# First MLP's short token block: high and low inputs side by side in one product of 512 columns

## Chip, cores and metric

The kernel runs on one core of a Trainium2 chip. The metric is the device time of one execution in microseconds (us). The kernel before was timed three times: 840.6 us median, 839.95 lowest, 841.95 highest.

## What is computed

The inputs are q, k, v of 4 batches, 8 heads, 576 positions and 64 channels, and four weight matrices. Retention comes first; its output is 2304 tokens by 512 channels. Two MLPs follow, each with 2048 hidden units and no bias. Cut to what matters:

```
scores = (q @ k.T) / 8                      # per batch and head
ret    = scores * decay                     # gamma[h] ** (i - j) for i >= j, else 0
x      = (ret @ v), heads side by side      # [2304, 512]
h = x @ w_in;   g = softplus(h);               x = g @ w_out     # first MLP, 512 -> 2048 -> 512
h = x @ w_in2;  g = h * sigmoid(1.702 * h);  out = g @ w_out2    # second MLP
```

Everything is float32. TensorE gets each operand as a high part (the value rounded to float32r) and a low part (what the rounding left), and a product of two operands is the sum of three: high times high, low times high, high times low.

## The kernel before

**Blocks and slices.** The first MLP goes over five blocks of tokens: the first 512 tokens of batches 0, 1 and 2, then a short block `"t"` of 256 tokens (the last 64 of each of the four batches), then the first 512 of batch 3. A block goes over 16 slices of 128 hidden units. Below, "slice n" is slice n of the short block, 0 to 15, unless another block is named.

**One slice** (`run_first`, L213 to L292). `mm1` makes the slice's hidden values `ph` (128 hidden units by the block's tokens, one PSUM bank, two of them in turn): four steps `kd` over the 512 channels, and in each the three products high weight by high input, low weight by high input, high weight by low input. ScalarE takes softplus of `ph` into `g` (L260, a tile with one buffer), casts it to the high part `gh` (L265, helper at L94), and VectorE makes the low part `gl = g - gh` (L267, helper at L99). `mm2` multiplies the slice into the block's four output banks `y` (four steps `e`, three products each, in the order high-high, high-low, low-high). All these products are issued at L211.

**Order.** The order of the instructions of each engine is written out by hand (`tc.manual_schedule`), and each engine takes its instructions in that order. With LAG = 2 one pass of the loop at L269 is: `mm1` of slice n, `start` (softplus), then `mm2` of slice n - 2, within which the cast to `gh` of slice n stands after step e = 0 and `gl` of slice n after e = 2. Where a block begins (slice 0), the inputs are first split into `xh` and `xl` (`split_block`, four casts on ScalarE, then four subtractions on VectorE), and one more `mm2` of the block ahead runs in front of the first `mm1`. So in the order of TensorE, `mm1` of slices 14 and 15 of the short block is followed by `mm2` of 13 and 14, and then by the first `mm1` of batch 3's block.

**Side work.** Four times in a pass, `side()` (a small accumulator; `pre`, ending at L1267, sets its rates) lets other work issue one step: in `mm1` after kd = 1 and after kd = 3, in `mm2` after e = 1 and after e = 3. In the short block this is `sums_steps` (L744 on), which prepares the second MLP's weights: a unit reads 512 KB of weights, forms four sums and stores 1024 KB of high and low parts. It has four steps: **A**, two 256-column sums on VectorE (L728, L729 or L736, L737); **B**, two more (L730, L731 or L738, L739), the issue of the read two units ahead, and the cast of the first two sums on ScalarE; **C**, their low part on VectorE and the cast of the other two; **D**, the low part of those and the issue of the store by SyncE. The rate is 0.66 steps a call, so two units take three slices. Their order against the slices repeats every three slices. Each tile of these steps (`whole`, `sum`, `sum_halves`) has two buffers, so a cast in B waits for the store of two units ago to land. In slice 15 the rate is 0.

- Between the `gl` of slices 3, 6, 9, 12 and that of the slice behind them stand C and D ahead of `start`, and A behind it.
- Between the `gl` of slices 4, 7, 10, 13 and the next stand B and C ahead of `start`, and D behind it.
- Between the `gl` of slices 5, 8, 11 and the next stand A and B ahead of `start` (C follows the next `gl`).

**End of a block.** `done` (L1273 to L1279) copies each `y` bank out of PSUM, alternately on ScalarE and VectorE, and SyncE stores it. For the short block this happens in `mm2` of its slice 15, which runs right after `mm1` of slice 1 of batch 3's block.

```python
    for i, cur in enumerate(work):           # L269, shortened to the steady case
        g = start(cur, mm1(cur))
        for e in mm2(behind.pop(0)):
            if e == 0:
                rest = split(cur, g)
            if e == 2:
                rest()
            if e in (1, 3):
                side()
```

Of the kernel before, what the change touches and what calls it, by code (L numbers as in the profile page):

```python
# [7 lines left out]
F32 = mybir.dt.float32  # L8
F32R = mybir.dt.float32r
U32 = mybir.dt.uint32  # L10
AF = mybir.ActivationFunctionType
ALU = mybir.AluOpType
# [3 lines left out]
P = 128  # L16
T = 512
C0 = 256
ENDS = 320
LAG = 2  # L20
# [13 lines left out]
def kernel(  # L34
# [36 lines left out]
    nc = tc.nc  # L71
# [5 lines left out]
    KD = DM // P  # L77
# [8 lines left out]
    xp = ctx.enter_context(tc.tile_pool(name="xp", bufs=1))  # L86
    tp = ctx.enter_context(tc.tile_pool(name="tp", bufs=1))
# [4 lines left out]
    def hi(eng, dst, src):  # L92
        if eng == "a":
            nc.scalar.copy(dst, src)  # L94
        else:
            nc.vector.tensor_copy(dst, src)

    def lo(dst, src, h):
        nc.vector.tensor_tensor(out=dst, in0=src, in1=f32(h), op=ALU.subtract)  # L99
# [108 lines left out]
    def passes(out_ap, pairs, first, last):  # L208
        k = len(pairs)
        for i, (l, r) in enumerate(pairs):  # L210
            nc.tensor.matmul(out_ap, l, r, start=first and i == 0, stop=last and i == k - 1)  # L211

    def run_first(work, ws, get_x, side, done, pre, post):  # L213

        ts, ys = {}, {}
        behind, late = [], []

        def mm1(it):  # L220
            key, n, f = it
            xh, xl = get_x(key)
            w = ws(f, 0)
            ph = ps_h.tile([P, T], F32, tag="h", name="ph")
            for kd in range(KD):
                wh, wl = (w[:, j, kd * P:(kd + 1) * P] for j in range(2))
                passes(
                    ph[:, 0:n],
                    [(wh, xh[:, kd, 0:n]), (wl, xh[:, kd, 0:n]), (wh, xl[:, kd, 0:n])],
                    kd == 0, kd == KD - 1)  # L230
                if kd % 2:
                    while late:
                        late.pop()()
                    side()
            return ph[:, 0:n]

        def mm2(it):
            key, n, f = it
            w = ws(f, 1)
            gh, gl = ts.pop(it)  # L240
            first, last = f == 0, f == NF - 1
            if first:
                ys[key] = [ps_y.tile([P, T], F32, tag="y", name="y") for _ in range(KD)]
            for e in range(KD):
                c = slice(e * P, (e + 1) * P)
                wh, wl = w[:, 0, c], w[:, 1, c]
                for i, pair in enumerate([(wh, gh), (wh, gl), (wl, gh)]):
                    passes(ys[key][e][:, 0:n], [pair], first and i == 0, last and i == 2)
                    if i < 2:
                        yield None  # L250
                if last:
                    done(key, n, e, ys[key][e])
                yield e
            if last:
                ys.pop(key)
            post(key, f)

        def start(it, ph):
            g = tp.tile([P, T], F32, tag="g", name="g", bufs=1)[:, 0:it[1]]
            nc.scalar.activation(g, ph, AF.Softplus)  # L260
            return g

        def split(it, g):
            gh, gl = (tp.tile([P, T], F32R, tag="gg", name=nm, bufs=2 * LAG + 2)[:, 0:it[1]] for nm in ("gh", "gl"))
            hi("a", gh, g)  # L265
            ts[it] = gh, gl
            return lambda: lo(gl, g, gh)  # L267

        for i, cur in enumerate(work):  # L269
            pre(*cur)  # L270
            behind.append(cur)
            if cur[2] == 0 and i:
# [3 lines that stand above are left out]
                late.append(split(cur, start(cur, mm1(cur))))  # L276
                continue
            g = start(cur, mm1(cur))
            if i == len(work) - 1:
                split(cur, g)()  # L280
                continue
            if len(behind) <= LAG:
                late.append(split(cur, g))
                continue
# [7 lines that stand above are left out]
        return (step for it in behind for step in mm2(it))  # L292

    with tc.manual_schedule():
# [3 lines left out]
        tokens = {k: B * TAIL if k == "t" else T for k in order}  # L298
# [12 lines left out]
        xs = {}  # L311

        def x_tiles(key, layer):
            xs[layer, key] = [xp.tile([P, KD, T], F32R, tag="x8", name=g, bufs=2) for g in ("xh", "xl")]

        def split_x(key, layer, src, kd, cols=None):

# [6 lines left out]
        def split_block(key, layer, src):  # L324
            x_tiles(key, layer)
            for late in [split_x(key, layer, src, kd) for kd in range(KD)]:
                late()
# [4 lines left out]
        with ExitStack() as consts, ExitStack() as right, ExitStack() as second:  # L332
# [297 lines left out]
            for _ in range(WARM):  # L630
# [3 lines left out]
                out=mask[:, 0:2, :].rearrange("p u j -> p (u j)"), in_=mask[:, 0:2, :].rearrange("p u j -> p (u j)"),  # L634
# [33 lines left out]
            w1_gen = convert_first(units, slots, w1_raw, w1_tiles, w1_loaded, made)  # L668

            x_tiles(order[0], 1)  # L670
            for i, _ in enumerate(first_batch()):
                if i == 9:
# [10 lines left out]
            def side():  # L683
                for s in (side_gen, conv):
                    s["acc"] += counts.pop(0) if counts and s is conv else s["rate"]
                    while s["acc"] >= 1.0:
                        s["acc"] -= 1.0
                        next(s["g"], None)
# [580 lines left out]
            def post(key, f):  # L1269
                if key == order[-1] and 3 <= f < NF - 2:  # L1270
                    next(loads)

            def done(key, n, e, y):  # L1273
                c = e % 2 * n if 2 * n <= T else 0
                if not c:
                    y_out["t"] = tp.tile([P, T], F32, tag="yb", name="yb", bufs=3)
                yb = y_out["t"][:, c:c + n]
                hi("v" if e % 2 else "a", yb, y[:, 0:n])
                nc.sync.dma_start(out=y1[key][e], in_=yb)  # L1279

            work = [(k, tokens[k], f) for k in order for f in range(NF)]
            run_second(run_first(work, w1, lambda k: xs[1, k], side, done, pre, post))


# [74 lines left out]
```

## Time and profile before

| what | value |
|---|---|
| median of three runs (lowest, highest) | 840.6 us (839.95, 841.95) |
| the profiled execution's own time | 840.94 us |
| its span, first to last instruction | 839.2 us |
| TensorE busy | 826.9 us, 99% of the span |
| VectorE, ScalarE, GpSimd busy | 569.1, 401.2, 94.9 us (68%, 48%, 11%) |
| mean granted TensorE clock | 0.998 |
| DMA, mean over the span | 259 GB/s |

Busy times are of one profiled execution, whose own time is 0.34 us above the median of the runs; between its span and its time lie 1.7 us. The short block is worked on from about 327 to 381 us of the span. "Idle before" in a row is the time that the engine stood still just ahead of the instruction, with the instruction or transfer that ended it. Matmul rows overlap, since matmuls are pipelined: their pace is read from one start to the next.

### The profile page before, as it was taken

What the parts mean: (1) busy time and instruction counts of PE and PEld (TensorE: products, weight loads), DVE (VectorE), ACT (ScalarE), POOL (GpSimd) and SP (SyncE); (2) the same over time, 40 slices, a digit from 0 to 9 for tenths busy, and PEclk for the clock granted to TensorE, in tenths of its full rate; (3) what the DMA queues carried; (4) which work ended last, traced back from release to release, by engine and by line L of the source; (5) the groups of instructions that cost most, each with busy time, mean ns of one, the idle gap of its engine ahead of it and who ended that gap; (6) DMA issues with size and microseconds to landing.
All of it is one profiled execution on the core that took longest, in us unless ns stands there. A gap on an engine that the chain in (4) does not pass through costs nothing.

```text
span 839.2 us, 17129 instructions
## 1 busy us (share of the span) xinstructions
PE 826.9 (99%) x6898; PEld 749.4 (89%) x6899; DVE 569.1 (68%) x1160; ACT 401.2 (48%) x786; POOL 94.9 (11%) x178
## 2 busy tenths in 40 slices
PE   8999999999999999999999999999999999999997
PEld 5788788888888788998888899999999999999997
DVE  3999996676665764775543767787778777866622
ACT  5665644434454434455244555555555555544321
POOL 3200001121111111000010111211111111111100
PEclk9999999999999999999999999999999999999999
DMA  8966325887787775899996677887798779766610
GB/s 345 407 260 242 119 88 194 266 287 270 232 264 280 236 237 179 307 354 370 417 382 209 233 268 251 304 308 252 267 331 299 258 267 346 265 239 234 217 55 26
DMA packets 64479, 217.53 MB, mean 259 GB/s; under 512 B 6416, under 2 KB 21648, under 8 KB 52112
## 3 DMA queue, kind: packets, MB, share of 16 engines
q0 software_dynamic: 20704, 116.40, 40.1%
q1 hardware_dynamic: 43536, 99.78, 32.5%
q8 instruction: 54, 0.88, 0.4%
q10 hardware_dynamic: 160, 0.26, 0.1%
q14 instruction: 25, 0.20, 0.1%
HBM read 157.70 MB, written 58.72 MB: 258 GB/s over the span
## 4 chain that ended last, share of the span: by engine, by line
PE 87%; DVE 7%; DMA 2%; issue 1%; ACT 1%; SPq 0%; DVEq 0%; ACTq 0%
PE ph L211 22%; PE y L211 22%; PE ph L876 20%; PE m L876 18%; PE ps_so L468 3%; PE y L876 3%; DMA w_kqv<-kqv 1%; DMA odec<-outdecay 1%; DVE wa L110 1%; DVE wa L105 1%; DVE wa L104 1%; DVE w L99 0%; DVE yb L948 0%; DVE ga L99 0%; DVE sv L516 0%
## 5 line engine op out<-in xcount | busy, mean ns | idle before, releaser
L211 PE MATMUL y<-gh,w 128*128 128x512 f32 (+1 forms) x640 | 195.6, 371 | 0.0
L211 PE MATMUL ph<-xh,w 128*128 128x512 f32 (+1 forms) x640 | 183.5, 371 | 0.9 <-ACT xh L94 0.6
L211 PEld LDWEIGHTS y<-gh,w 128*128 128x128 f32 x640 | 116.8, 189 | 19.9
L211 PEld LDWEIGHTS ph<-xh,w 128*128 128x128 f32 x640 | 115.0, 189 | 21.7 <-ACT xh L94 1.0
L211 PE MATMUL y<-gl,w 128*128 128x512 f32 (+1 forms) x320 | 118.0, 369 | 0.0
L211 PE MATMUL ph<-xl,w 128*128 128x512 f32 (+1 forms) x320 | 118.0, 369 | 0.0
L876 PE MATMUL m<-w,ga 128*128 128x256 f32 x768 | 117.3, 283 | 0.5 <-DVE yb L948 0.5
L876 PE MATMUL ph<-xo_c,w 128*128 128x256 f32 x768 | 108.3, 283 | 0.2 <-DVE he L1104 0.2
L876 PE MATMUL ph<-xo,w 128*128 128x256 f32 x768 | 105.5, 283 | 0.1
L876 PEld LDWEIGHTS m<-w,ga 128*128 128x128 f32 x768 | 102.9, 190 | 1.1 <-PE ph L876 1.1
L876 PEld LDWEIGHTS ph<-xo_c,w 128*128 128x128 f32 x768 | 97.8, 189 | 1.9 <-DVE he L1104 1.1
L876 PEld LDWEIGHTS ph<-xo,w 128*128 128x128 f32 x768 | 97.6, 189 | 1.1 <-DVE ho L1142 0.9
L99 DVE TENSOR_TENSOR gl<-g,gh 128x512 fp32r<-128x512 f32 (+1 forms) x80 | 50.8, 635 | 64.6 <-ACT gh L94 64.6
L876 PE MATMUL m<-w,gb 128*128 128x256 f32 x576 | 89.7, 283 | 0.0
L260 ACT ACTIVATE g<-ph 128x512 f32<-128x512 f32 (+1 forms) x80 | 44.1, 551 | 90.8 <-PE ph L211 86.5
L876 PEld LDWEIGHTS m<-w,gb 128*128 128x128 f32 x576 | 78.1, 191 | 0.0
L211 PEld LDWEIGHTS ph<-xl,w 128*128 128x128 f32 x320 | 60.4, 189 | 10.2 <-DVE xl L99 0.2
L211 PEld LDWEIGHTS y<-gl,w 128*128 128x128 f32 x320 | 60.4, 189 | 9.6
L99 DVE TENSOR_TENSOR ga<-g,ga 128x512 fp32r<-128x512 f32 x72 | 46.9, 685 | 9.1 <-ACT ga L94 9.1
L94 ACT CAST ga<-g 128x512 fp32r<-128x512 f32 x72 | 44.7, 621 | 15.4 <-PE y L876 7.9
L104 DVE TENSOR_SCALAR wa<-wa 128x512 uint32<-128x512 uint32 (+1 forms) x53 | 25.9, 489 | 32.4 <-ACT wa L179 32.4
L94 ACT CAST gh<-g 128x512 fp32r<-128x512 f32 (+1 forms) x80 | 46.3, 579 | 2.4
(144 smaller groups left out, 1097.0 us busy)
## 6 DMA issues: line engine op xcount, KB each, us to landing
w<-sums_in POOLq DMA_DIRECT2D x32, 1024.0 KB, 5.5
w<-sums_out POOLq DMA_DIRECT2D x32, 1024.0 KB, 7.7
raw<-kqv SPq DMA_DIRECT2D x24, 512.0 KB, 5.8
w<-kept POOLq DMA_DIRECT2D x12, 1024.0 KB, 8.3
w_raw<-w_in SPq DMA_DIRECT2D x16, 512.0 KB, 9.3
w_raw<-w_out SPq DMA_DIRECT2D x16, 512.0 KB, 9.7
raw<-w_in POOLq DMA_DIRECT2D x16, 512.0 KB, 5.7
raw<-w_out POOLq DMA_DIRECT2D x16, 512.0 KB, 5.4
```

What stands on the lines that cost most here:

```text
L94: nc.scalar.copy(dst, src)
L99: nc.vector.tensor_tensor(out=dst, in0=src, in1=f32(h), op=ALU.subtract)
L104: nc.vector.tensor_single_scalar(out=u, in_=u, scalar=3, op=ALU.logical_shift_left)
L105: nc.vector.scalar_tensor_tensor(out=u, in0=w[:, :, 1], scalar=0x80000000, in1=u, op0=ALU.bitwise_and, op1=ALU.bitwise_or)
L110: nc.vector.scalar_tensor_tensor(out=u, in0=w[:, :, 0], scalar=29, in1=u, op0=ALU.logical_shift_right, op1=ALU.bitwise_or)
L211: nc.tensor.matmul(out_ap, l, r, start=first and i == 0, stop=last and i == k - 1)
L260: nc.scalar.activation(g, ph, AF.Softplus)
L468: nc.tensor.matmul(z[halves[m], o, at:at + D], l[halves[g]], rhs[halves[g]], start=clear[o][m], stop=True, skip_group_check=True)
L876: nc.tensor.matmul(out_ap, l, r, start=clear, stop=True, skip_group_check=True)
```

## The change

For the short block, whose 256 high and 256 low input columns fit side by side into one 512-column tile, the high weight meets both in one product, and the low weight meets the high columns as before: two products in place of three, in `mm1` and in `mm2`. Columns 0 to 255 of the PSUM bank then hold high-high plus low-high, columns 256 to 511 high-low, and the two halves are added once per bank: in `start` by a ScalarE copy of the upper half into `h` and a VectorE addition, with softplus now reading `h`; in `done` likewise for the four output banks, all four copies on ScalarE. The input block and each slice's `gh`, `gl` take one tile each instead of two.

```diff
@@ mm1
-                passes(
-                    ph[:, 0:n],
-                    [(wh, xh[:, kd, 0:n]), (wl, xh[:, kd, 0:n]), (wh, xl[:, kd, 0:n])],
-                    kd == 0, kd == KD - 1)
+                if 2 * n <= T:
+                    passes(ph[:, 0:2 * n], [(wh, xh[:, kd, 0:2 * n])], kd == 0, False)
+                    passes(ph[:, 0:n], [(wl, xh[:, kd, 0:n])], False, kd == KD - 1)
+                else:
...
@@ mm2
-                for i, pair in enumerate([(wh, gh), (wh, gl), (wl, gh)]):
-                    passes(ys[key][e][:, 0:n], [pair], first and i == 0, last and i == 2)
-                    if i < 2:
+                y = ys[key][e]
+                if 2 * n <= T:
+                    parts = [(y[:, 0:2 * n], wh, ts_both), (y[:, 0:n], wl, gh)]
+                else:
+                    parts = [(y, wh, gh), (y, wh, gl), (y, wl, gh)]
+                for i, (o, l, r) in enumerate(parts):
+                    passes(o, [(l, r)], first and i == 0, last and i + 1 == len(parts))
+                    if i + 1 < len(parts):
                         yield None
@@ start and split
-            g = tp.tile([P, T], F32, tag="g", name="g", bufs=1)[:, 0:it[1]]
-            nc.scalar.activation(g, ph, AF.Softplus)
+            n = it[1]
+            g = tp.tile([P, T], F32, tag="g", name="g", bufs=1)
+            if 2 * n <= T:
+                g, h = g[:, 0:n], g[:, n:2 * n]
+                hi("a", h, ph[:, n:2 * n])
+                nc.vector.tensor_tensor(out=h, in0=ph[:, 0:n], in1=h, op=ALU.add)
+                nc.scalar.activation(g, h, AF.Softplus)
+            else:
+                nc.scalar.activation(g, ph, AF.Softplus)
...
+            n, both = it[1], None
+            if 2 * n <= T:
+                both = tp.tile([P, T], F32R, tag="gg", name="gb", bufs=2 * LAG + 2)
+                gh, gl = both[:, 0:n], both[:, n:2 * n]
+            else:
...
@@ x_tiles
-            xs[layer, key] = [xp.tile([P, KD, T], F32R, tag="x8", name=g, bufs=2) for g in ("xh", "xl")]
+            both = 2 * tokens[key] <= T
+            x = [xp.tile([P, KD, T], F32R, tag="x8", name=g, bufs=2) for g in (("xb",) if both else ("xh", "xl"))]
+            xs[layer, key] = [x[0], x[0][:, :, T // 2:]] if both else x
@@ done
-                hi("v" if e % 2 else "a", yb, y[:, 0:n])
+                if 2 * n <= T:
+                    hi("a", yb, y[:, n:2 * n])
+                    nc.vector.tensor_tensor(out=yb, in0=y[:, 0:n], in1=yb, op=ALU.add)
+                else:
+                    hi("v" if e % 2 else "a", yb, y[:, 0:n])
```

## Rows read from the trace of the kernel before

**Rows 1.** Windows, 334 to 372 us: PE, PEld, DVE, ACT, POOL busy; clock; DMA.

```profile
334.00:372.00 38.00, 38.00 (x319) 38.00 (x318) 26.39 (x60) 18.63 (x42) 0.00 (x0) 1.00 0.88 332
```

**Rows 2.** The chain of waits: start us, us, what.

```profile
334.65 1.44 PE y L211 x12
...
387.33 2.72 PE ph L211 x12
```

**Rows 3.** Timeline of PE (start us, us, instruction).

```profile
343.24 0.28 PE L211 MATMUL y<-gl,w 128*128 128x256 f32 x1
...
374.80 0.63 PE L211 MATMUL ph<-xh,w 128*128 128x512 f32 x2
...
384.45 0.39 PE L211 MATMUL y<-gh,w 128*128 128x512 f32 x1
```

**Rows 4.** Groups by line and shape: busy us, mean ns of one, idle before.

```profile
L94 ACT CAST gh<-g 128x256 fp32r<-128x256 f32 x16 | 6.5, 407 | 0.5
...
L260 ACT ACTIVATE g<-ph 128x256 f32<-128x256 f32 x16 | 6.1, 381 | 6.3 <-PE ph L211 4.1 <-DVE yb L96 1.5 <-DVE gl L99 0.6
```

**Rows 5.** Groups by line and shape, second MLP: copies and additions that read PSUM.

```profile
L1104 DVE TENSOR_TENSOR he<-ph,m 128x256 f32<-128x256 f32 x32 | 13.6, 425 | 1.0 <-ACT m L1090 1.0
...
L1090 ACT COPY m<-ph 128x256 f32<-128x256 f32 x32 | 12.0, 374 | 17.0 <-PE ph L876 17.0
```

**Rows 6.** Timeline of DVE, slices 3 to 6 (gl) and the sums between.

```profile
341.37 0.42 DVE L99 TENSOR_TENSOR gl<-g,gh 128x256 fp32r<-128x256 f32 x1 [0.74 <-ACT gh L94]
341.71 1.28 DVE L99 TENSOR_TENSOR sum_halves<-sum,sum_halves 128x512 fp32r<-128x512 f32 x2
342.92 0.42 DVE L728 TENSOR_TENSOR sum<-whole 128x256 f32<-128x256 f32 x1
...
343.71 0.42 DVE L99 TENSOR_TENSOR gl<-g,gh 128x256 fp32r<-128x256 f32 x1
344.05 0.42 DVE L730 TENSOR_TENSOR sum<-whole 128x256 f32<-128x256 f32 x1
...
344.72 1.47 DVE L99 TENSOR_TENSOR sum_halves<-sum,sum_halves 128x512 fp32r<-128x512 f32 x2
346.21 0.43 DVE L99 TENSOR_TENSOR gl<-g,gh 128x256 fp32r<-128x256 f32 x1
...
347.00 0.43 DVE L737 TENSOR_TENSOR sum<-whole,sum 128x256 f32<-128x256 f32 x1
...
348.84 0.43 DVE L99 TENSOR_TENSOR gl<-g,gh 128x256 fp32r<-128x256 f32 x1 [0.74 <-ACT gh L94]
```

**Rows 7.** Timeline of ACT in the same stretch.

```profile
344.84 0.62 ACT L94 CAST sum_halves<-sum 128x512 fp32r<-128x512 f32 x1 [0.39 <-DVE sum L731]
345.36 0.38 ACT L260 ACTIVATE g<-ph 128x256 f32<-128x256 f32 x1
345.77 0.41 ACT L94 CAST gh<-g 128x256 fp32r<-128x256 f32 x1
...
347.46 0.62 ACT L94 CAST sum_halves<-sum 128x512 fp32r<-128x512 f32 x1 [1.28 <-DVE sum L737]
347.99 0.38 ACT L260 ACTIVATE g<-ph 128x256 f32<-128x256 f32 x1
```

**Rows 8.** Timeline of ACT and DVE, turn to batch 3's block.

```profile
373.45 2.18 ACT L94 CAST xh<-xf 128x512 fp32r<-128x512 f32 x4
...
374.09 2.50 DVE L99 TENSOR_TENSOR xl<-xf,xh 128x512 fp32r<-128x512 f32 x4
...
382.83 0.41 DVE L96 COPY yb<-y 128x256 f32<-128x256 f32 x1
```

**Rows 9.** DMA issues, 320 to 400 us: KB each, median us to landing.

```profile
sums_in<-sum_halves SPq DMA_DIRECT2D x6, 1024.0 KB, 5.8
sums_out<-sum_halves SPq DMA_DIRECT2D x5, 1024.0 KB, 6.4
```

**Rows 10.** Timeline of ACT: its longest wait for a store here.

```profile
357.25 0.62 ACT L94 CAST sum_halves<-sum 128x512 fp32r<-128x512 f32 x1 [3.60 <-DMA sums_out<-sum_halves]
```

More of the change, by code (lines that the diff above doesn't have):

```diff
@@ L226, in mm1 @@
                 wh, wl = (w[:, j, kd * P:(kd + 1) * P] for j in range(2))
-                passes(
-                    ph[:, 0:n],
-                    [(wh, xh[:, kd, 0:n]), (wl, xh[:, kd, 0:n]), (wh, xl[:, kd, 0:n])],
-                    kd == 0, kd == KD - 1)
+                if 2 * n <= T:
+                    passes(ph[:, 0:2 * n], [(wh, xh[:, kd, 0:2 * n])], kd == 0, False)
+                    passes(ph[:, 0:n], [(wl, xh[:, kd, 0:n])], False, kd == KD - 1)
+                else:
+                    passes(
+                        ph, [(wh, xh[:, kd]), (wl, xh[:, kd]), (wh, xl[:, kd])], kd == 0, kd == KD - 1)
                 if kd % 2:
@@ L234, in mm1 @@
                     side()
-            return ph[:, 0:n]
+            return ph
         def mm2(it):
@@ L239, in mm2 @@
             w = ws(f, 1)
-            gh, gl = ts.pop(it)
+            gh, gl, ts_both = ts.pop(it)
             first, last = f == 0, f == NF - 1
@@ L258, in start @@
         def start(it, ph):
-            g = tp.tile([P, T], F32, tag="g", name="g", bufs=1)[:, 0:it[1]]
-            nc.scalar.activation(g, ph, AF.Softplus)
+            n = it[1]
[7 more added lines that the diff above has]
+                nc.scalar.activation(g, ph, AF.Softplus)
             return g
         def split(it, g):
-            gh, gl = (tp.tile([P, T], F32R, tag="gg", name=nm, bufs=2 * LAG + 2)[:, 0:it[1]] for nm in ("gh", "gl"))
+            n, both = it[1], None
[3 more added lines that the diff above has]
+            else:
+                gh, gl = (tp.tile([P, T], F32R, tag="gg", name=nm, bufs=2 * LAG + 2) for nm in ("gh", "gl"))
             hi("a", gh, g)
-            ts[it] = gh, gl
+            ts[it] = gh, gl, both
             return lambda: lo(gl, g, gh)
```

## The prediction

> **What bounds the kernel now.** The page's busy shares come first: TensorE 99%, and in a window inside the short block it works 38.00 of 38.00 us at a granted clock of 1.00, the upper of its two levels (2.4 GHz), with the DMA engines 88% busy [rows 1]. So the products set the pace there, and a shorter stream of products shortens the kernel unless something behind TensorE becomes late. The chain of waits gives the pace: twelve products of 256 columns take 1.44 us, or 120.0 ns each, and twelve of 512 take 2.72 us, or 226.7 ns [rows 2]. What could become late is the chain softplus, cast, subtraction, which feeds each slice's `mm2`; VectorE is busy only 26.39 of the 38 us [rows 1], which looks like room. The timelines of VectorE and ScalarE correct that look: what counts is one slice's chain, since `g` has one buffer and both engines take their work in the written order.
>
> **The products.** In each `mm1` and each `mm2` twelve products of 256 columns become four of 512 and four of 256: 12 x 0.120 = 1.440 us become 4 x 0.2267 + 4 x 0.120 = 1.387 us, 0.053 us less. There are 32 of them, so at most 1.7 us is to be had. The arithmetic columns are the same; what goes is the fixed part of 128 products, 2 x 120.0 - 226.7 = 13.3 ns each. The weight loads that go with them lie beside products and are worth nothing by themselves.
>
> The Trainium skill ("TensorE: Matmul & The Clock Gate", section "Back-to-back issue gap") gives an isolated product N / 2.4 + 2.5 ns, so by its figure the 128 products would be worth an estimated 0.3 us. The spacing of the rows, 226.7 and 120.0 ns, has 13.3 ns in that place, and the rows decide.
>
> **The chain of a slice, before.** `gl` of slices 3, 4, 5 and 6 starts at 341.37, 343.71, 346.21 and 348.84 [rows 6]: steps of 2.34, 2.50 and 2.63 us, together 7.47 for three slices. TensorE needs 3 x 2 x 1.44 = 8.64 for them [rows 2]. The chain has 1.17 us of room in three slices, and here, late after a wait, it is catching up: these are its own shortest steps.
>
> **The chain, after.** In `start` a copy of the upper half and an addition come ahead of softplus. Neither exists before in the first MLP; the nearest rows are a ScalarE copy of 256 columns out of PSUM, 374 ns, and a VectorE addition of 256 columns out of PSUM and SBUF, 425 ns [rows 5]. I take these. Softplus reads SBUF instead of PSUM; I take its 381 ns, and as the other end the 407 ns of the cast that reads SBUF [rows 4], 0.3 us over twelve slices. A hop between engines is 0.03 us: the sum at 347.00 lasts 0.43 and its cast starts at 347.46 [rows 6, 7]. From the start of the addition to the start of `gl` is therefore 0.425 + 0.381 + 0.407 + 3 x 0.03 = 1.30 us. When the addition can start depends on the side steps ahead of it in VectorE's order. Counted from the last `gl`:
>
> - After slices 3, 6, 9, 12 (C, D ahead): the two subtractions start 0.34 later and hold VectorE 342.92 - 341.71 = 1.21 [rows 6]; the copy is ready by then. 0.34 + 1.21 + 1.30 = 2.85.
> - After slices 4, 7, 10, 13 (B, C ahead): the cast of C starts 344.84 - 343.71 = 1.13 later, ScalarE is free 0.52 after that [rows 6, 7], then copy and hop: 1.13 + 0.52 + 0.40 + 1.30 = 3.35.
> - After slices 5, 8, 11 (A, B ahead): the cast of B starts 347.46 - 346.21 = 1.25 later, again 0.53, copy and hop: 1.25 + 0.53 + 0.40 + 1.30 = 3.48.
>
> Together 9.68 us for three slices, against 3 x 2 x 1.387 = 8.32 of TensorE. The chain becomes the bound, by 1.36 us in three slices. VectorE's 16 additions, at the 0.34 us in which `gl` lets the next row start, would only lift its 26.39 us by 5.4; the shares of busy time do not show this.
>
> **From where it binds.** `gl` of slice 3 moves later by copy, addition and two hops, 0.86, to 342.23, and is done 0.45 later, at 342.68. Its first reader was the product at 343.24 [rows 3]; the new first product holds `gl` too, 0.12 earlier, and nine `mm1` and `mm2` ahead have saved 0.48: TensorE is there at 342.64. So from slice 3 on TensorE waits for the chain. Eleven slices on, `gl` of slice 14 starts at 342.23 + 3 x 9.68 + 2.85 + 3.35 = 377.47, done at 377.92. `mm2` of 14 began at 374.80 - 1.44 = 373.36 before [rows 3]; now it ends at 377.92 + 1.39 = 379.31. The two PSUM banks of `ph` cost nothing more: `mm1` of a slice waits for the addition two slices back, which precedes that slice's `gl` by 1.30, about one `mm1`.
>
> **The turn to batch 3.** Behind slice 15's chain stand the four casts to `xh` on ScalarE and the subtractions to `xl` on VectorE [rows 8]. After `gl` of 14 come D's subtraction and the addition: 377.47 + 0.34 + 0.60 = 378.41 for the addition (half of 1.21 for one subtraction); softplus and cast end 1.27 later, 379.68; the first `xh`, 0.62 like other casts of 512 columns [rows 7], is there with its hop at 380.33; the first `xl` begins there and takes 2.50 - 3 x 0.605 = 0.69 (four take 2.50, one every 1.21 / 2) [rows 6, 8], with its hop at 381.05. The third product needs it 0.45 after the start, at 380.78, so 0.27 more is waited. The block starts as if at 380.60 where it started at 374.80 [rows 3]: 5.8 later. From there TensorE has always been fed, so nothing is regained; `mm2` of slice 15 gives 0.05 back.
>
> **Stores of the sums.** The cast of B behind slices 5, 8, 11 needs the store of two units ago. That leaves when D's subtraction ends, 0.34 + 1.28 = 1.62 after a `gl` [rows 6]; the cast comes 2.85 - 1.62 + 3.35 + 1.25 = 5.8 us later. Landing took a median of 6.4 (`sums_out`, the units in question from slice 9 on) and 5.8 us [rows 9]. At two places 0.6 us is short, so the ends are 0 (the sums now come at 8.64/9.68 of their rate, which relieves the DMA engines) and 1.2; I take 0.6. One wait of the longest kind, 3.60 [rows 10], would be the far end.
>
> **The rest.** `done` of the short block makes four copies and four additions of two and two copies. Its last row ended at 383.24 [rows 8]; the fourth bank is next written nine products after 384.45, at 386.49 [rows 3], 3.2 us of cover for two copies and additions, 1.6; uncovered it would cost up to that. SyncE's stores of the block and the next read of weights behind them shift by as much, and no product waits for them. One tile instead of two for the input lets batch 3's `xh` go into the other buffer; its casts are held by ScalarE's order, so 0.
>
> **Sum.** 840.94 + 5.8 - 0.05 + 0.6 = 847.3 us, against this profiled execution; the median of the runs shown is 0.34 lower. The forecast's own range is 845.5 (no wait for stores, and the late `xh` and `xl` half hidden) to 849.5 (two waits twice as long, and the slower softplus).
>
> **Rivals.** *Faster: the chain stays hidden.* The copy and the addition find both engines idle, for instance where ScalarE now waits for stores, `mm2` runs two slices behind and never notices, and all of 1.7 us is kept: 839.2. For it speak VectorE's 12 idle us in 38; against it the steps of 2.34 to 2.63, which are no idle time but one slice's chain. It decides whether three slices take under 8.32 us rather than 9.68. *No change: only the turn waits.* The loop keeps up, but TensorE, 1.6 us early, meets casts 0.86 us later: the first `xh` ended at 373.45 + 0.62 = 374.07, now 374.93, where TensorE stands ready at 374.80 - 30 x 0.053 = 373.2. It waits 1.7, and 1.7 was won: 840.9. The hidden chain with the skill's 2.5 ns per product would also end there, at 840.6. *Slower still: stores set the pace.* Later stores hold later casts, one wait of 3.60 in place of 0.6: 850.3.
>
> **Chances.** Forecast 0.73, stores 0.06, no change 0.11, faster 0.10. A measurement of this kernel tells about 0.2%, 1.7 us, from no change. The range must leave out no more than 2 in 10, so it reaches to the case of no change: 840.9 to 850.3, leaving out the faster case.
>
> **What would show it.** Right: PE rows in the short block with gaps ended by DVE `gl`, VectorE additions of 425 ns behind copies of 374 ns, `gl` starts 9.7 us apart over three slices, the first product of batch 3's block near 380.5. Products still spaced 226.7 and 120.0 ns show the 1.7 us as issued but not kept. Wrong: a busy TensorE through the short block, or `gl` starts 8.3 us apart.

## The result, and the profile of the changed kernel

The changed kernel takes 848.12 us, median of six runs (847.2 to 849.08), against 840.28 us for six runs of the kernel before beside it: a ratio of 1.0087, 95% interval 1.0073 to 1.0101. Forecast were 847.3 us, slower. The profiled execution has a span of 846.1 us against 839.2.

The window inside the short block, columns as in [rows 1]:

```profile
334.00:372.00 38.00, 34.60 (x186) 27.93 (x185) 26.58 (x63) 19.74 (x46) 0.00 (x0) 1.00 0.81 293
```

TensorE, busy all 38.00 us before, now stands still for 3.40 of them, at the same granted clock of 1.00. VectorE is busy for 26.58 us, hardly more than the 26.39 of before, with 63 instructions in place of 60: in the same time less of the block is done. The timeline of PE names what it waits for (the rows shown have a wait, from slice 0 to the turn, with some left out at each `...`; `gb` is now the tile that holds `gh` and `gl`, L271 the addition):

```profile
334.73 0.62 PE L211 MATMUL y<-gb,w 128*128 128x512 f32 x2 [0.33 <-DVE yb L96]
341.65 1.66 PE L211 MATMUL ph<-xb,w 128*128 128x512 f32 x8 [0.65 <-DVE g L271]
...
347.94 1.66 PE L211 MATMUL ph<-xb,w 128*128 128x512 f32 x8 [0.32 <-DVE g L271]
...
351.46 1.66 PE L211 MATMUL ph<-xb,w 128*128 128x512 f32 x8 [0.48 <-DVE g L271]
...
378.74 1.68 PE L211 MATMUL y<-gb,w 128*128 128x512 f32 x8 [1.70 <-DVE gb L99]
...
381.08 0.73 PE L211 MATMUL ph<-xh,w 128*128 128x512 f32 x2 [0.67 <-ACT xh L94]
```

`mm1` of a slice waits for the addition two slices back, which frees its bank; `mm2` of slice 14 waits 1.70 us for that slice's `gl`, and batch 3's block 0.67 us for `xh`. (A wait of the weight load ahead of a product stands in the rows of PEld, TensorE's weight loads, and not here, so these do not add up to the whole.)

The timeline of VectorE over the same three slices as [rows 6], L271 the addition, L99 with 256 columns the low part:

```profile
342.52 0.42 DVE L99 TENSOR_TENSOR gb<-g,gb 128x256 fp32r<-128x256 f32 x1 [0.92 <-ACT gb L94]
342.86 1.28 DVE L99 TENSOR_TENSOR sum_halves<-sum,sum_halves 128x512 fp32r<-128x512 f32 x2
344.06 0.42 DVE L271 TENSOR_TENSOR g<-ph,g 128x256 f32<-128x256 f32 x1
...
345.40 0.43 DVE L99 TENSOR_TENSOR gb<-g,gb 128x256 fp32r<-128x256 f32 x1
...
347.46 0.42 DVE L271 TENSOR_TENSOR g<-ph,g 128x256 f32<-128x256 f32 x1 [0.36 <-ACT g L94]
...
348.81 0.43 DVE L99 TENSOR_TENSOR gb<-g,gb 128x256 fp32r<-128x256 f32 x1 [0.32 <-ACT gb L94]
...
350.98 0.42 DVE L271 TENSOR_TENSOR g<-ph,g 128x256 f32<-128x256 f32 x1 [0.29 <-ACT g L94]
352.33 0.43 DVE L99 TENSOR_TENSOR gb<-g,gb 128x256 fp32r<-128x256 f32 x1 [0.93 <-ACT gb L94]
```

From `gl` to `gl` it is 2.88, 3.41 and 3.52 us, 9.81 for three slices (forecast 2.85, 3.35, 3.48; before 2.34, 2.50, 2.63). Ahead of each `gl` VectorE stands or fills 0.9 us with other work while ScalarE does softplus and cast; ahead of the addition it does the same for the copy. Where the two low parts of the sums stand between a `gl` and the next addition, as from 342.86 to 344.06, it is VectorE's own queue that holds the addition.

The block's first product in the timeline of PE, before and now:

```profile
327.43 0.40 PE L211 MATMUL ph<-xh,w 128*128 128x256 f32 x2
...
326.18 2.97 PE L211 MATMUL ph<-xb,w 128*128 128x512 f32 x16
```

From there to the first product of batch 3's block it took 374.80 - 327.43 = 47.37 us before [rows 3] and takes 381.08 - 326.18 = 54.90 now, 7.53 more. The chain of waits carries this on to the end of the two `mm1` that follow (the block's first piece and the piece behind those two `mm1`, before and now):

```profile
327.59 2.87 PE ph L211 x24
...
380.43 1.43 PE y L211 x12
...
326.35 1.42 PE ph L211 x8
...
387.13 1.40 PE y L211 x8
```

That is 52.84 us before and 60.78 now, so the block costs 7.9 us more, 0.4 of it inside the two `mm1`. The spans differ by 6.9 us, since this execution came to the block 1.25 us earlier, with the same code ahead of it; the 0.2 us left over lie behind the block.

### The profile page after: what moved, and what is told of

The parts are those of the page before. It is cut to its first block, busy times and chain, and to the rows that moved or that the text cites. A ratio compares the mean times of both kernels' runs of the same rounds, so it can differ in the third digit from the quotient of the medians.

```text
span 846.1 us, 16904 instructions
## 1 busy us (share of the span) xinstructions
PE 829.3 (98%) x6771; PEld 742.0 (88%) x6771; DVE 576.3 (68%) x1178; ACT 408.1 (48%) x804; POOL 95.0 (11%) x178
## 4 chain that ended last, share of the span: by engine, by line
PE 81%; DVE 9%; ACT 3%; DMA 3%; issue 2%; SPq 0%; DVEq 0%; ACTq 0%
PE ph L897 20%; PE ph L211 19%; PE y L211 18%; PE m L897 18%; PE ps_so L489 3%; PE y L897 3%; DMA w_kqv<-kqv 1%; DMA w_raw<-w_in 1%; DVE wa L110 1%; DVE wa L105 1%; DVE g L271 1%; ACT g L272 1%; DVE sum_halves L99 1%; ACT gb L94 1%; DVE gb L99 1%
## 5 line engine op out<-in xcount | busy, mean ns | idle before, releaser
L211 PE MATMUL y<-gh,w 128*128 128x512 f32 x512 | 170.2, 393 | 0.0
L211 PE MATMUL ph<-xh,w 128*128 128x512 f32 x512 | 159.9, 393 | 1.5 <-ACT xh L94 1.2
L211 PEld LDWEIGHTS ph<-xh,w 128*128 128x128 f32 x512 | 94.9, 188 | 22.5 <-ACT xh L94 2.0
L211 PEld LDWEIGHTS y<-gh,w 128*128 128x128 f32 x512 | 95.7, 188 | 20.2 <-DVE yb L96 0.2
L211 PE MATMUL ph<-xl,w 128*128 128x512 f32 x256 | 99.9, 390 | 0.0
L211 PE MATMUL y<-gl,w 128*128 128x512 f32 x256 | 99.7, 390 | 0.0
L99 DVE TENSOR_TENSOR gl<-g,gh 128x512 fp32r<-128x512 f32 x64 | 44.1, 688 | 57.4 <-ACT gh L94 57.2
L274 ACT ACTIVATE g<-ph 128x512 f32<-128x512 f32 x64 | 38.0, 594 | 86.8 <-PE ph L211 84.6
L99 DVE TENSOR_TENSOR gb<-g,gb 128x256 fp32r<-128x256 f32 x112 | 43.9, 421 | 23.8 <-ACT gb L94 23.3
L99 DVE TENSOR_TENSOR ga<-g,ga 128x512 fp32r<-128x512 f32 x72 | 46.9, 685 | 9.1 <-ACT ga L94 9.1
L94 ACT CAST gb<-g 128x256 fp32r<-128x256 f32 x112 | 45.4, 407 | 0.8
```

## The experiments

Two theories of the loss stood against each other at first. **The chain**: copy and addition lengthen each slice's way from `ph` to `gl`, in engines that take their work in the written order. **The products and the output banks**: TensorE loses by products of 512 and 256 columns in turn, or by the additions at the block's end. Each run is compared with runs of the kernel before on the same chip, whose medians were 840.86 us beside the first four, 840.99 beside the next three and 840.57 beside the last four. A ratio and its 95% interval are taken from all the runs, not from the two medians.

### The chain alone, without the change of the products

```diff
@@ start, in the kernel before
+            if 2 * n <= T:
+                g, h = g[:, 0:n], g[:, n:2 * n]
+                hi("a", h, ph)
+                nc.vector.tensor_tensor(out=h, in0=ph, in1=h, op=ALU.max)
+                nc.scalar.activation(g, h, AF.Softplus)
...
```

> The kernel before, all its products as they were, with only a ScalarE copy and a VectorE operation of 256 columns put ahead of each softplus of the short block (the maximum of ph and its copy, which is ph). Chain theory: the chain of a slice is the bound whatever the products are, so three slices take about 9.8 us here too and the time is that of the changed kernel, 848 us within 1. Rival, the products: if the loss comes from products of 512 and 256 columns taking turns, or from the output banks being added, this kernel stays at 840 to 841.

Measured: 847.9 us, 1.0082 (1.0066 to 1.0097). The low parts of slices 3 to 6, in the timeline of VectorE, 9.81 us from the first to the last:

```profile
342.90 0.42 DVE L99 TENSOR_TENSOR gl<-g,gh 128x256 fp32r<-128x256 f32 x1 [0.92 <-ACT gh L94]
345.79 0.43 DVE L99 TENSOR_TENSOR gl<-g,gh 128x256 fp32r<-128x256 f32 x1
349.19 0.43 DVE L99 TENSOR_TENSOR gl<-g,gh 128x256 fp32r<-128x256 f32 x1 [0.32 <-ACT gh L94]
352.71 0.42 DVE L99 TENSOR_TENSOR gl<-g,gh 128x256 fp32r<-128x256 f32 x1 [0.92 <-ACT gh L94]
```

Two small operations a slice make as large a loss as the whole change, within the intervals, with every product as it was. The rival falls.

### The products alone, without the addition

```diff
@@ start, in the changed kernel
-            if 2 * n <= T:
...
+            nc.scalar.activation(g, ph[:, 0:n], AF.Softplus)
```

> The changed kernel without the copy and the addition in front of softplus; it leaves out the high-weight by low-input part of the short block's hidden values (softplus reads the lower half of the bank alone). Products, output banks and tiles are those of the change. Chain theory: TensorE is the bound again, the 1.7 us of the 128 saved products come out, 838.6 us, or up to 840.3 if the turn to batch 3's block takes them back. Rival, the products or the output banks: 846 to 848.

Measured: 840.54 us, 1.0008 (0.9990 to 1.0026), just above the 838.6 to 840.3 expected. No product of the short block waits, and the additions at the block's end cost nothing that can be seen. But the saving does not show in the time either, and the chain of waits says why:

```profile
335.15 1.42 PE ph L211 x8
...
370.50 2.82 PE y L211 x16
373.31 5.55 PE ph L211 x24
```

From 335.15 to 370.50 there are 25 pieces, 1.414 us each: 0.026 less than the 1.440 before, not 0.053. The 32 pieces give 0.8 us, less than these runs can resolve.

### Each half by itself

The second layer's products only:

```diff
-                if 2 * n <= T:
-                    passes(ph[:, 0:2 * n], [(wh, xh[:, kd, 0:2 * n])], kd == 0, False)
...
+                passes(ph[:, 0:n], [(wh, xh[:, kd, 0:n]), (wl, xh[:, kd, 0:n]), (wh, xl[:, kd, 0:n])],
+                       kd == 0, kd == KD - 1)
@@ start
+            nc.scalar.activation(g, ph[:, 0:n], AF.Softplus)
```

> Only the second layer's products side by side (mm2, with one addition per output bank at the block's end); mm1, its input tiles taking one buffer, and softplus straight from PSUM as before. Chain theory: no link is added to a slice's chain, half of the saving comes out, 16 x 0.053 = 0.85 us: 839.4 us, within 0.2% of before. Rival, the output banks: their copies and additions cost 1 us or more, 841 or above.

Measured: 841.37 us, 1.0007 (0.9994 to 1.0020): no difference, and the 0.85 us is not there. The saving of 16 x 0.026 = 0.4 us would be within the interval. The median lies in the rival's range, 841 or above, but so near to the 840.86 of the kernel before that these runs cannot tell the two apart. The profiled execution does not show the rival: TensorE waits 0.20 us there for `gl` of slice 14, and by the chain of waits the two `mm1` after the turn take 5.76 us in place of 5.47, both ahead of the output banks' additions. Gain or loss of this half stays undecided.

The first layer's products only, with copy and addition:

```diff
-                if 2 * n <= T:
-                    parts = [(y[:, 0:2 * n], wh, ts_both), (y[:, 0:n], wl, gh)]
-                else:
-                    parts = [(y, wh, gh), (y, wh, gl), (y, wl, gh)]
+                y = y[:, 0:n]
+                parts = [(y, wh, gh), (y, wh, gl), (y, wl, gh)]
...
@@ done
-                if 2 * n <= T:
-                    hi("a", yb, y[:, n:2 * n])
-                    nc.vector.tensor_tensor(out=yb, in0=y[:, 0:n], in1=yb, op=ALU.add)
-                else:
-                    hi("v" if e % 2 else "a", yb, y[:, 0:n])
+                hi("v" if e % 2 else "a", yb, y[:, 0:n])
```

> Only the first layer's products side by side, with the copy and the addition; mm2 and the output banks as before. Chain theory: the loss of the whole change, 848 us within 1, since the chain sets the pace and mm2's longer products lie in TensorE's idle time. Rival, each half of the change costs its share: 844.

Measured: 848.7 us, 1.0093 (1.0076 to 1.0111). The whole loss belongs to the half that puts the addition into the chain.

### Two buffers for g

```diff
-            g = tp.tile([P, T], F32, tag="g", name="g", bufs=1)
+            g = (cpool["cp"] if 2 * n <= T else tp).tile([P, T], F32, tag="g", name="g", bufs=2 if 2 * n <= T else 1)
...
```

> The changed kernel with two buffers of g in the short block (taken from the pool that the sums use), so that no slice's copy waits for the slice before to be done with g. Theory, written order: the copy is held by the casts of the sums ahead of it on ScalarE, and the addition by the subtractions ahead of it on VectorE, not by the buffer, so the three-slice step stays at 9.8 us and the time at 848 us within 1. Rival, the one buffer of g holds the chain: three slices come near TensorE's 8.4 us and the time falls to 842 or below.

Measured: 848.19 us, 1.0086 (1.0063 to 1.0109), with `gl` of slices 3 and 6 at 344.72 and 354.53, 9.81 us. The written order holds the chain, not the buffer.

### The sums taken out of the short block

```diff
-                        conv.update(g=sums_gen["g"], rate=0.66)
+                        conv.update(g=sums_gen["g"], rate=0.0)
...
-                        conv["rate"] = 0.75
+                        conv["rate"] = 1.7
```

> The changed kernel with all steps of the sums taken out of the short block and issued in batch 3's block at 1.7 steps a call in place of 0.75. Theory, interleaving: with nothing between them copy, addition, softplus, cast and subtraction of a slice take about 0.37 + 0.42 + 0.42 + 0.41 + 0.42 and hops, 2.2 us, under TensorE's 2.83 a slice; no product of the short block waits from slice 2 on, and block start to batch 3's first product takes about 46.5 us as in the kernel without the addition, against 54.9 in the changed kernel. Rival, the chain is too long by itself: the stretch stays above 50 us. The total is not the question here, since batch 3's block then carries all the stores.

In the short block the theory holds. VectorE's timeline, with `gl` 2.83 us behind `gl`, the pace of TensorE:

```profile
340.54 0.42 DVE L271 TENSOR_TENSOR g<-ph,g 128x256 f32<-128x256 f32 x1 [1.05 <-ACT g L94]
341.89 0.43 DVE L99 TENSOR_TENSOR gb<-g,gb 128x256 fp32r<-128x256 f32 x1 [0.93 <-ACT gb L94]
343.37 0.42 DVE L271 TENSOR_TENSOR g<-ph,g 128x256 f32<-128x256 f32 x1 [1.05 <-ACT g L94]
344.72 0.43 DVE L99 TENSOR_TENSOR gb<-g,gb 128x256 fp32r<-128x256 f32 x1 [0.92 <-ACT gb L94]
```

The chain of waits gives the stretch as 326.87 to 374.02, 47.2 us where 46.5 were expected, with one wait of 0.32 us for an output copy of the block ahead, and none after it. So the chain by itself fits; with the sums interleaved in this order it does not. Taking the sums out also takes their load from VectorE and ScalarE, so this run alone does not tell order from load; the next ones do. The total, 878.62 us in one run, shows the other side: in batch 3's block TensorE then waits for softplus, up to 8.45 us at a time, behind casts of the sums that wait for their stores.

### The chain spread over two passes

The order of one slice's links in the short block, in words (the edit itself is longer):

```
before:  mm1 -> copy, addition, softplus -> (e = 0) cast -> (e = 2) subtraction
now:     mm1 -> copy -> (e = 0) addition -> (e = 2) softplus -> next mm1: (kd = 1) cast -> (kd = 3) subtraction
```

> The changed kernel with the chain of a slice spread over its pass and the next one: copy right after mm1, addition after e = 0 of mm2, softplus after e = 2, cast after kd = 1 and subtraction after kd = 3 of the next mm1, each with a step of the sums between it and the link it needs. No work is added or left out. Theory, written order: no engine waits for a link just issued, ScalarE and VectorE have room, TensorE is the bound; with the pair of a 512 and a 256 product at 354 ns as seen without the addition, 0.8 us of the saving comes out, 839.5 to 841 us. Rival, the two added operations cost by their load or their PSUM reads: 844 or more.

Measured: 843.13 us, 1.0031 (1.0017 to 1.0044), a miss by 2 us on the slow side, though 5 us better than the change. In VectorE's timeline `gl` of slice 3 is at 342.74 and that of slice 6 at 351.61: 8.87 us for three slices, 0.94 less than in the changed kernel and still above TensorE's 6 x 1.414 = 8.48. Its first product of the short block to wait for `gl` does so at 340.15, right behind the start of the sums:

```profile
340.15 1.66 PE L211 MATMUL y<-gb,w 128*128 128x512 f32 x8 [0.40 <-DVE gb L99]
...
342.74 0.42 DVE L99 TENSOR_TENSOR gb<-g,gb 128x256 fp32r<-128x256 f32 x1
...
351.61 0.42 DVE L99 TENSOR_TENSOR gb<-g,gb 128x256 fp32r<-128x256 f32 x1
```

That start was the next question.

### The first reads of the sums earlier

The same edit in three kernels: the changed one, the one before (a control), the spread one.

```diff
@@ sums_steps
-                for _ in range(5):
-                    yield
                 read(0)
                 yield
                 read(1)
                 yield
+                for _ in range(5):
+                    yield
```

> The changed kernel with the first two reads of the sums issued five steps earlier, ahead of the stores of batch 2's block; the sums themselves keep their steps. Theory: in the changed kernel the chain starts late in slice 3, because VectorE stands 2.98 us before the first sum until the read lands, and as everything behind is chain-bound that wait is part of the loss; without it gl of slice 3 comes up to 2.9 us earlier and the time is about 845.2 us. Rival, the loss is the slower steps alone and the wait is hidden as it was before the change: 848 us, no change.

> The kernel before with the same two reads five steps earlier, as the control. Theory: TensorE is the bound there and the chain has room, so the 3.1 us that VectorE waits are hidden: 840 to 841.5 us, no change. Rival, the earlier reads help by themselves, by relieving the DMA engines or the turn: 839 or below.

> The spread chain with the reads ahead. Theory: the spread chain alone takes 8.87 us for three slices against TensorE's 8.48 and was 2.1 us slower than before, of which the late start is a part; with the reads ahead it starts up to 2.9 us earlier and the remaining 0.13 us a slice is covered by that lead, so TensorE is the bound to the turn: 840.3 to 841.3 us. Rival, something else than the chain costs the 2.1 us: 843.

Measured: 845.3 us for the changed kernel, 1.0052 (1.0035 to 1.0069); 840.26 us for the control, 0.9998 (0.9981 to 1.0015); 840.62 us for the spread kernel, 0.9996 (0.9980 to 1.0012). In the changed kernel with this edit TensorE's first wait for an addition comes at 358.25 in place of 341.65, six slices later (`mm1` of slice 11 in place of 5):

```profile
334.72 0.62 PE L211 MATMUL y<-gb,w 128*128 128x512 f32 x2 [0.28 <-DVE yb L96]
358.25 1.68 PE L211 MATMUL ph<-xb,w 128*128 128x512 f32 x8 [0.30 <-DVE g L271]
```

The same wait was worth 2.8 us where the chain bounds and nothing that can be seen where TensorE does. With both edits no product of the short block waits, and the time is that of the kernel before. In the window of [rows 1] TensorE is then busy for 38.00 of 38.00 us, with VectorE at 31.80 and ScalarE at 23.77 us, more than the 26.58 and 19.74 of the changed kernel. So it was the order of the links and their late start that cost the time, not the load on these two engines.

### Fewer sums in the short block

```diff
@@ in the spread kernel with the reads ahead
-                        conv.update(g=sums_gen["g"], rate=0.66)
+                        conv.update(g=sums_gen["g"], rate=0.55)
...
-                        conv["rate"] = 0.75
+                        conv["rate"] = 0.86
```

> As the spread chain with the reads ahead, and the sums at 0.55 steps a call in the short block and 0.86 in batch 3's, in place of 0.66 and 0.75. Theory: the chain takes less than TensorE's 2.83 us a slice, the short block keeps the 0.8 us of its products, 839.8 to 840.8 us, if batch 3's block still carries its sums in its room. Rival, the sums moved to batch 3's block make it wait for stores, as at 1.7 steps a call: 842 or more.

Measured: 843.38 us, 1.0037 (1.0019 to 1.0056). The rival holds: in the profiled execution TensorE waits in batch 3's block, 1.4 us for softplus and 1.3 us for `gl`, behind casts that wait for stores. No version was found that beats the kernel before, and with 0.8 us to be had one could hardly be told from it.

## Why the prediction was right, and where its sum was off

**What bounds.** Right: the chain of a slice and not TensorE, from the written order, with VectorE idle a third of the time. The chain alone reproduces the loss, the products alone have none. The forecast named one buffer of `g` beside the written order; with two buffers the loss stays, so the buffer has no part in it. One sign came out otherwise: the forecast looked for gaps of TensorE ended by `gl` and took the wait for a bank of `ph` to cost nothing more. From slice 5 on the gaps of PE in the short block end with the addition (L271), which frees the bank, and `gl` ends only that of slice 14. The addition stands 1.35 us ahead of `gl` in the same chain, so the pace is the same.

**The steps.** Right within 0.06 us each. What was taken from the nearest rows measured this, in the groups by line and shape of the short block:

```profile
L271 DVE TENSOR_TENSOR g<-ph,g 128x256 f32<-128x256 f32 x16 | 6.8, 422 | 6.4 <-ACT g L94 6.4
L272 ACT ACTIVATE g<-g 128x256 f32<-128x256 f32 x16 | 6.7, 418 | 11.1 <-DVE g L271 11.1
...
L94 ACT COPY g<-ph 128x256 f32<-128x256 f32 x16 | 5.9, 369 | 5.8 <-PE ph L211 4.6 <-DVE gb L99 1.1
```

Copy and addition are within 5 ns of [rows 5]; softplus out of SBUF takes 418 ns, beyond even the slower end of 407. From `gl` of slice 3 to that of slice 14, at 378.25, it takes 378.25 - 342.52 = 35.73 us, 0.49 more than forecast.

```profile
378.25 0.43 DVE L99 TENSOR_TENSOR gb<-g,gb 128x256 fp32r<-128x256 f32 x1 [0.92 <-ACT gb L94]
```

**From where it binds.** Here the sum was off most. `gl` of slice 3 came 342.52 - 326.18 = 16.34 us after the block's first product, against 341.37 - 327.43 = 13.94 before: 2.40 later, where 0.86 was forecast for one slice's copy and addition. The chain of waits shows what was left out:

```profile
327.78 0.38 ACT g L94
...
330.05 0.38 ACT g L94
330.46 0.44 DVE g L271
330.92 0.42 ACT g L272
331.34 0.47 ACT yb L94
331.83 2.05 DMA y<-yb
333.98 0.69 DVE yb L96
335.37 3.74 DMA whole<-whole_in
339.33 0.44 DVE sum L749
```

The chains of slices 0 and 1 already hold ScalarE, and with it the copy of batch 2's first output bank, whose buffer a later copy needs. SyncE takes its stores and then the first read of the sums in order, so the reads are issued later against the block. SyncE's timeline, before (with the first sum in VectorE's) and now:

```profile
335.36 0.83 SPq L752 DMA_DIRECT2D whole<-whole_in  x2
339.08 0.42 DVE L728 TENSOR_TENSOR sum<-whole 128x256 f32<-128x256 f32 x1 [3.12 <-DMA whole<-whole_in]
...
335.37 0.82 SPq L773 DMA_DIRECT2D whole<-whole_in  x2
```

That is 7.93 us after the block's first product before and 9.19 now, 1.26 later. The first sum starts 339.33 - 326.18 = 13.15 us after it, against 339.08 - 327.43 = 11.65 before: 1.5 later. The forecast took that start as fixed. Moving the reads earlier takes 2.8 us off the changed kernel and nothing that can be seen off the one before, which shows that the wait for the read is on the path only after the change; that 1.26 us of the delay comes by way of the output copy is read from this chain and was not tried alone.

**The stores.** Forecast 0.6 us, measured none: in the short block no cast waits for a store any more. The stores land in 4.5 and 4.6 us where it was 5.8 and 6.4 [rows 9], with the DMA engines 81% busy in the window in place of 88%. That the slower pace of the sums is the reason, the forecast's case of 0, was not tried alone:

```profile
sums_in<-sum_halves SPq DMA_DIRECT2D x6, 1024.0 KB, 4.5
sums_out<-sum_halves SPq DMA_DIRECT2D x4, 1024.0 KB, 4.6
```

**The turn.** From `gl` of slice 14 to batch 3's first product 381.08 - 378.25 = 2.83 us, forecast 2.86; the wait for `xl` inside the next two `mm1` costs 60.78 - 52.84 - 7.53 = 0.41, forecast 0.27.

**The sum.** Start 1.54 too little, steps 0.49 and turn 0.11 too little, stores 0.6 too much: 1.5 in all, and 6.4 (5.8 + 0.6) + 1.5 is the 7.9 us of this execution. The medians differ by 7.8. That 847.3 lies only 0.8 below 848.12 is in part luck: the 0.6 for the stores offsets part of what was missing, and the sum starts from 840.94, which is 0.66 above the median of the runs beside the changed kernel.

**The products.** Forecast were 0.053 us a piece and 1.7 us at most. Without the chain they show 0.026, so the rival of a hidden chain, priced at 839.2, could have reached 840.1 at best. By the spacing of [rows 2], 256 more columns take 226.7 - 120.0 = 106.7 ns, so the 3072 columns of a piece take 1.280 us at this clock (2.4 GHz): the fixed part was 0.160 / 12 = 13.3 ns each, and is 0.134 / 8 = 16.8 ns where 512 and 256 columns take turns. That it would stay 13.3 was the wrong step. The Trainium skill ("TensorE: Matmul & The Clock Gate", section "Back-to-back issue gap") has 2.5 ns in that place for an isolated product; no row here comes near it.

## What to carry to other kernels

An operation that is cheap beside an engine's idle time can still set the pace if it becomes a link in a per-slice chain of two engines that take turns in a fixed order: measure the chain from one of its links to the next, where it is catching up, and add the new links there, before looking at busy shares. When such a chain passes the pace of the engine that bounds, waits that were hidden in it, such as the landing of a first read, join the path. Fewer, wider products are worth only their fixed part: by the rows of before 13.3 ns for each product less, of which 0.026 / 4 = 6.5 ns came out here.

## What the hardware showed that was not expected

Products of 512 and 256 columns in turn take 353.5 ns a pair (1.414 / 4), 6.8 more than the 226.7 + 120.0 they take each among its own kind [rows 2]; why stays open. Softplus of 256 columns takes 418 ns out of SBUF against 381 out of PSUM [rows 4]. Waits of up to 1.70 us left the granted clock at 1.00 (2.4 GHz) in the changed kernel, from 326 to 460 us. With the sums in batch 3's block, in one run, where TensorE waits 8.45 and 8.03 us at a time, its mean from 372 to 460 us is 0.88, between the two levels of 2.4 and 1.2 GHz (that kernel's windows; the first is the short block):

```profile
326.00:372.00 46.00, 45.68 (x254) 39.19 (x253) 14.33 (x33) 19.21 (x48) 0.00 (x0) 1.00 0.08 29
372.00:460.00 88.00, 65.90 (x264) 52.14 (x263) 50.04 (x106) 31.65 (x58) 4.94 (x10) 0.88 0.94 358
```
